# GpSimd's pattern additions of an attention kernel: int16 words with a constant instead of int32 words with a broadcast operand, and another written order

## The chip, the core and the metric

The kernel runs on one core of a Trainium2 chip. The time is the device time of one execution in microseconds, and the figure of a kernel is the median over its runs. The core has five engines that work side by side, each through its own list of instructions: TensorE (PE; its weight loads are shown apart as PEld), VectorE (DVE), ScalarE (ACT), GpSimd (POOL) and SyncE (SP), which here issues all transfers. [...]

## What is computed

The inputs are a matrix `x` of 2048 rows and 512 columns in bf16, and weights. Its normalised rows go through an attention block of 32 heads and, beside it, a gated feed-forward block; both are added to `x`:

```python
xn = _layernorm(x, axis=-1)
qkv = (xn @ wqkv).reshape(B, S, 3, H, Dh)          # H = 32, Dh = 16
p = _softmax(jnp.einsum("bhqd,bhkd->bhqk", q, k) * (Dh ** -0.5), axis=-1)
o = jnp.einsum("bhqk,bhkd->bhqd", p, v)
gate = xn @ W_gate;  gate = gate * (gate > 0)       # F = 1792
return x + o_rows @ wo + (gate * (xn @ W_up)) @ W_down
```

Most of the work is the attention: 32 heads with 2048 x 2048 scores each, whose exponentials are wanted.

## The kernel before, in words

**Tiling.** The scores are made transposed: 128 keys on the partitions and 512 queries along the free dimension, for four heads at a time. A block is 512 queries (`c4`, 4 of them) by eight heads (`gg`, 4 of them) by one half of these heads (`ee`, 2 of them), so there are 32 blocks, and each runs over 16 tiles of 128 keys (`kt`). One tile of keys in one block is four score tiles of 128 x 512 in PSUM. TensorE makes them, another engine makes exponentials of them in SBUF, and TensorE multiplies these with the values and sums over the keys (`pv_stream`, line 1255).

**Two ways to an exponential.** For a tile of keys that goes to ScalarE, two instructions of line 1376 each take two of the four score tiles (128 x 1024) through the exponential table. There are 720 of them, called units, and the program's order is told in units. The other way is `quad` (line 1323), for the tiles of keys that have a digit in `QUAD_AT` (line 67), 152 in all. There VectorE adds a bias to each score tile and rounds to int16 (line 1331, four times for one tile of keys, 608 in all); the scores have been scaled so that the bits of this integer, read as bf16, are about a power of two. That is the raw pattern, 128 x 2048 int16 words. Two more patterns are the raw one with 31 and with 81 added to each word (`SHIFTS`, line 105). All three go to TensorE as bf16, and their sum approximates the exponential.

**Who adds the shifts.** The digit in `QUAD_AT` is a mask over the two shifted patterns: a set bit gives it to GpSimd, a clear bit to VectorE. From the fourth row of the table on, rows alternate between `2...3..3..0..3..` (seven patterns for GpSimd) and `2...3..3..2..3..` (eight), until the last row (a 2 gives it one pattern, a 3 two, a 0 none). GpSimd makes 225 patterns, each in two pieces (`POOL_PIECES`, line 53), so line 1346 stands 450 times; VectorE makes the other 79 in one instruction each (line 1350). GpSimd's instruction looks at the int16 words in pairs, as int32 words, and adds a second operand, one int32 word per partition that is repeated along the row; that word holds the shift twice, as 31 x 65537 and 81 x 65537, and is made by two iotas (line 634).

```python
QUAD_AT = ("................", ".0....3.....2...", ".3...3...2...3..", "2...3..3..0..3..", "2...3..3..2..3..", ...)
SHIFTS = (0, 31, 81)
POOL_PIECES = 2
POOL_NS = 1900
```

**What else GpSimd does.** It multiplies the output of each block by the reciprocal of the softmax's sum (lines 1238 and 1243, 31 times) and does small things at the start.

**Buffers.** There are four buffers for raw patterns (`NRAW`) and five for shifted ones (`NPAT`), 16 for ScalarE's exponentials, and eight PSUM banks, of which four hold the scores of two units and four are shared by everything else.

**What sets the order.** The functions record operations in a graph (`Graph.op`, line 280) with what each reads and writes. The order on every engine is not found while the kernel is built: it is a table, packed in the text `PLAN` (line 123), which `Graph.run` (line 325) unpacks. For each of its 8245 places the table names the operation, and for operations that take a buffer, the buffer. Waits follow from reads, writes and buffers. One wait is added for the sake of SBUF: an operation marked `port` on GpSimd waits for the last VectorE operation marked `port` ahead of it in the table (line 365); VectorE's operations wait for none of GpSimd's in this way. Both line 1346 and line 1350 are marked. The durations that `Graph.op` is given (for a piece `POOL_NS / POOL_PIECES + 60`) belong to the planning of the table and decide nothing when the kernel is built.

Of the kernel before, what the change touches and what calls it, by code (L numbers as in the profile page):

```python
# [10 lines left out]
I32 = mybir.dt.int32  # L11
# [3 lines left out]
ALU = mybir.AluOpType  # L15

S = 2048
D = 512
H = 32
DH = 16  # L20
F = 1792
# [31 lines left out]
POOL_PIECES = 2  # L53
# [1375 lines left out]
```

## Time and profile before

| What | Value |
|---|---|
| median of 2 runs | 693.66 us (693.58 to 693.75) |
| the profiled execution | 690.92 us |
| its span | 689.1 us |
| TensorE's granted clock in it | 0.999 |
| busy: PE, PEld, DVE, ACT, POOL | 680.3, 355.1, 600.3, 669.8, 503.1 us |
| moved by the transfers | 35.87 MB, 52 GB/s over the span |

How to read it: the span runs from the first to the last instruction of the profiled execution, and its own time is a little longer. A busy time counts the moments in which at least one instruction of the engine was running, so two that overlap count once; the mean of one instruction in a group is its full duration, and can be longer than the time until the next one starts. In a group's row stand line, engine, operation, what it writes and reads, shape and count, then the busy time and the mean in ns, then how long the engine stood idle just before such instructions, and who ended that. The view of one line gives the shortest, the median and the longest duration, and who waited for the line. A timeline's row begins with start and length in us, and merges instructions that follow each other without a gap.

### The profile page before, as it was taken

The page shows a single profiled execution, that of the slowest core. Times are in us where ns is not written, and L with a number is a line of the kernel's source. Part 1 is how long each engine was busy: PE and PEld are TensorE (multiplying, and loading weights), DVE is VectorE, ACT ScalarE, POOL GpSimd, SP SyncE. Part 2 cuts the span into 40 slices and gives each one's busy share as a digit, 9 for nine tenths or more (in the row PEclk, how much of TensorE's full clock was granted, in tenths as well). Part 3 has the DMA queues.
Part 4 walks back from the last instruction along what each step waited for, and adds up shares of the span by engine and source line. Part 5 has one row for each costly group of instructions (what it writes and reads, how often), then busy time and mean ns, then how long its engine had stood idle before and what let it go on. Part 6 is the DMA issues. An engine that isn't in the chain of part 4 may idle for free.

```text
span 689.1 us, 45379 instructions
## 1 busy us (share of the span) xinstructions
PE 680.3 (99%) x22232; PEld 355.1 (52%) x20044; DVE 600.3 (87%) x1009; ACT 669.8 (97%) x733; POOL 503.1 (73%) x511
## 2 busy tenths in 40 slices
PE   8999999999999999999999999999999999999997
PEld 4455555554544555455544555555554455555553
DVE  9958899997999788999998787999899887988886
ACT  6999999999999999999999999999999999999994
POOL 3223669767878778968878787987878788696791
PEclk9999999999999999999999999999999999999999
DMA  7430121214111012111100104111110112131011
GB/s 215 54 74 15 51 85 31 62 44 116 35 53 45 22 53 74 40 49 46 51 25 26 29 20 118 31 43 44 44 32 22 30 58 57 61 86 31 20 30 59
DMA packets 55941, 35.87 MB, mean 52 GB/s; under 512 B 19336, under 2 KB 51784, under 8 KB 55752
## 3 DMA queue, kind: packets, MB, share of 16 engines
q1 hardware_dynamic: 55752, 32.97, 17.3%
q8 instruction: 165, 2.70, 1.6%
q14 instruction: 24, 0.20, 0.1%
HBM read 26.35 MB, written 2.35 MB: 42 GB/s over the span
## 4 chain that ended last, share of the span: by engine, by line
PE 88%; DVE 5%; ACT 4%; SPq 1%; DMA 1%; issue 0%; POOL 0%; DVEq 0%
PE ps L251 88%; ACT ring L1376 4%; DVE qd L1331 1%; DVE stats L725 1%; SPq L857 1%; DVE xn_sb L738 1%; DMA x_sb<-oT 1%; SPq L1247 0%; DMA x_sb<-in_A_x_dram 0%; DVE up_sb L1014 0%; DVE qd L1350 0%; DVE xnT L779 0%; DVE v_aug L874 0%; POOL rstd L720 0%; DVE mv L726 0%
## 5 line engine op out<-in xcount | busy, mean ns | idle before, releaser
L1376 ACT ACTIVATE ring<-ps 128x1024 bf16<-128x1024 f32 x720 | 663.5, 1100 | 3.8 <-PE ps L251 2.7
L1346 POOL TENSOR_TENSOR qd<-qd,ints 128x512 int32<-128x512 int32 x450 | 453.7, 1039 | 152.0 <-DVE qd L1350 101.8
L251 PE MATMUL ps<-qT,kT 64*32 64x512 bf16 x8192 | 451.6, 374 | 1.2 <-ACT ring L1376 0.3
L1331 DVE TENSOR_SCALAR qd<-ps 128x512 int16<-128x512 f32 x608 | 396.6, 686 | 56.9 <-PE ps L251 50.2
L251 PE MATMUL ps<-qd,v_aug 64*32 64x512 bf16 x3648 | 266.4, 375 | 0.4
L251 PE MATMUL ps<-ring,v_aug 64*32 64x512 bf16 x2880 | 241.9, 375 | 0.1
L1311 PEld LDWEIGHTS <-kT 64*32 64x32 bf16 x7732 | 158.9, 92 | 126.4 <-issue 34.2
L1283 PEld LDWEIGHTS <-v_aug 64*32 64x32 bf16 x4800 | 114.2, 91 | 79.0 <-issue 25.3
L251 PE MATMUL ps<-xnT,wgs 64*32 64x512 bf16 x1792 | 139.5, 375 | 0.1
L251 PE MATMUL ps<-xnT,wus 64*32 64x512 bf16 x1792 | 137.8, 374 | 0.0
L809 PEld LDWEIGHTS <-wus 64*32 64x32 bf16 x1792 | 43.5, 91 | 29.1 <-issue 6.7
L809 PEld LDWEIGHTS <-wgs 64*32 64x32 bf16 x1792 | 43.4, 91 | 29.1 <-issue 6.5
L251 PE MATMUL ps<-Wd,hT 64*32 64x512 bf16 x768 | 56.7, 375 | 0.5 <-DMA x_sb<-oT 0.5
L1350 DVE TENSOR_SCALAR qd<-qd 128x2048 int16<-128x2048 int16 x79 | 53.8, 693 | 2.6 <-PE ps L251 2.4
L809 PEld LDWEIGHTS <-hT 64*32 64x32 bf16 x1792 | 40.8, 92 | 26.1 <-issue 3.2
L1018 DVE SCALAR_TENSOR_TENSOR hT<-ps,up_sb 128x512 bf16<-128x512 f32 x56 | 38.4, 686 | 6.9 <-PE ps L251 6.1
L251 PE MATMUL ps<-Wk,hT 64*32 64x512 bf16 x512 | 43.9, 375 | 0.0
L251 PE MATMUL ps<-Wv,hT 64*32 64x512 bf16 x512 | 43.9, 375 | 0.0
L1014 DVE COPY up_sb<-ps 128x512 f32<-128x512 f32 x56 | 38.3, 685 | 2.2 <-PE ps L251 1.3
L251 PE MATMUL ps<-Wo_p,x_sb 64*32 64x512 bf16 x480 | 38.2, 375 | 0.0
L251 PE MATMUL ps<-xnT,Wq 64*32 64x512 bf16 x480 | 37.1, 375 | 0.0
L251 PE MATMUL ps<-xnT,Wk 64*32 64x512 bf16 x480 | 34.8, 374 | 0.2 <-DVE xnT L779 0.2
(72 smaller groups left out, 267.4 us busy)
## 6 DMA issues: line engine op xcount, KB each, us to landing
rb<-rec_scr SPq DMA_DIRECT2D x31, 256.0 KB
wus<-in_B_W_up_dram SPq DMA_DIRECT2D x38, 128.0 KB, 2.7
wgs<-in_B_W_gate_dram SPq DMA_DIRECT2D x38, 128.0 KB, 3.1
xr_sb<-in_A_x_dram SPq DMA_DIRECT2D x16, 128.0 KB, 3.1
out_dram<-xn_sb SPq DMA_DIRECT2D x16, 128.0 KB, 2.3
qT<-qf SPq DMA_DIRECT2D x120, 16.0 KB, 2.6
x_sb<-in_A_x_dram SPq DMA_DIRECT2D x8, 128.0 KB, 2.8
x_sb<-oT SPq DMA_DIRECT2D x60, 16.0 KB, 2.3
```

The lines of the kernel that those rows point to most:

```text
L251: return e.add_instruction(mybir.InstMatmult(name=e.bass.get_next_instruction_name(), engine=mybir.EngineType.PE, ins=[e.lower_ap(x), e.lo ...
L725: G.op("DVE", 580, lambda e, m=m: e.bn_stats(stats[:, m, :], xs(m)), reads=[t_xm[m]], writes=[t_st], prio=pr, order=last_xn if m == 4 else ())
L738: G.op("DVE", 320, lambda e, m=m, t=t_n: e.tensor_scalar(xn_sb[:, t.slot, :], xs(m), mv[:, m, 0:1], rstd[:, m:m + 1], op0=ALU.subtract, op ...
L809: e.ldweights(w()[rows, 32 * j:32 * j + 32], tile_position=(rows.start, 32 * j))
L1014: G.op("DVE", 603, lambda e: e.tensor_copy(up_sb[:, tup.slot, :], bank_of(tu)), reads=[tu], writes=[tup], prio=-590)
L1018: G.op("DVE", 603, lambda e: e.scalar_tensor_tensor(out=hT[:, th.slot, :], in0=bank_of(tg), scalar=0.0, in1=up_sb[:, tup.slot, :], op0=ALU ...
L1283: e.ldweights(vs(j), tile_position=(64 * half, 32 * j))
L1311: e.ldweights(ks(m), tile_position=(64 * half, 32 * m))
L1331: G.op("DVE", 601, lambda e, j=j, tx=tx: e.tensor_scalar(qd[:, tq.slot, 512 * j:512 * j + 512], ps[:, BANK[tx.slot], :], IBIAS[3], 0.0, op ...
L1346: G.op("POOL", POOL_NS / POOL_PIECES + 60, lambda e, x=x, n=n, c=slice(i * m, i * m + m): e.tensor_tensor(x().bitcast(I32)[:, c], raw().bi ...
L1350: G.op("DVE", 600, lambda e, n=n, x=x: e.tensor_scalar(x(), raw(), float(SHIFTS[n + 1]), None, op0=ALU.add), reads=[ti, tq], writes=[t], p ...
L1376: exp_ops[u] = G.op("ACT", 904, lambda e, tr=tr, k0=k0: e.activation(ring[:, tr.slot, :, :], ps[:, 4 * k0:4 * k0 + 2, :], ACTF.Exp, scale= ...
```

## The change

Two things change together. The table of order in `PLAN` is another one, with the same number of places (8245); the text of it is left out here. And the instruction of line 1346 is another: an addition of a constant that is part of the instruction, over int16 words in pieces of 1024, where it was an addition of two tensors over int32 words in pieces of 512. The number of pieces (two for a pattern, 450 in all), their bytes, their waits and `QUAD_AT` stay, as do the iotas of the shift words, which nothing reads any more.

```diff
 PLAN_OPS = 8245
 PLAN = (
...
                 if mask >> n & 1:
-                    m = 1024 // POOL_PIECES
+                    m = 2048 // POOL_PIECES
                     for i in range(POOL_PIECES):
-                        G.op("POOL", POOL_NS / POOL_PIECES + 60, lambda e, x=x, n=n, c=slice(i * m, i * m + m): e.tensor_tensor(
-                            x().bitcast(I32)[:, c], raw().bitcast(I32)[:, c], shift[:, n:n + 1].to_broadcast([128, m]), ALU.add),
+                        G.op("POOL", POOL_NS / POOL_PIECES + 60, lambda e, x=x, n=n, c=slice(i * m, i * m + m): e.tensor_scalar(
+                            x()[:, c], raw()[:, c], float(SHIFTS[n + 1]), None, op0=ALU.add),
                             reads=[ti, tq, t_shift], writes=[t] if i == 0 else [], joins=[] if i == 0 else [t], prio=u, name="p3", port=True)
```

More of the change, by code (lines that the diff above doesn't have):

```diff
@@ new lines @@
+    "@vfKu3L%hhDfg{Mig#~Y4Y?rSeLdd;Q@UKN+fR*6r8Exn(!N%#r;4wpK07GfyD>M!8C&W?f_TK~Qapsb%@ybzy79IyA8~1nys&f<Yq_3MJhwOHw!6jmT!Fc*_nskEu{~w3_qlEE3vO>L-m;&Qy4-vw"
+    "O)($QGSd!I1M!-%oo;GsD8nu5$yjdO^ahreaKj@~e|Q66`_Hl$atSTa?J!vTh~;u~A;9=Xk<Reumtv-g?H}V6Bjo0`rbUW0*AzwHx>X;~a^1Yo<qFHgy0xo(X73|x6O!Dj^n>YEa)S|eu|_xV>58Sc"
+    "VUXz*({plxP{LHisxI9sAsKzU22E2fa|~<6ZBqrq4*Mn3^F}<R)<~V~QoL_+ahO8I`|vI{LT)JJwM1IRj3N*Vjcb`ky7a$dCZ{eFQ8!{|TB&=LNvV=_4KqB)6{grFYiQts&P`zO(5B4e^&RbRit~td"
+    "iup+KVufzKYhRi15VB+%ntO<FN^3kaa!g9sJ(f0#hlxi_N-`WFuIRZ(ZY<0;-lZG#TTu*QuuS?7fO+fN2WJf*B{_5@Nz;>cr!G8Wq!bx$%h658i|x%s^(dzM<^FPS<}m{#ElASfk@;#FWjkAhST}bO"
@@ new lines @@
+    "3JXadCd-^DrgJPEErY#!c$gVDSROVi(FO>keiSbf*y%0r3dM~WFezT>BJFa6*$qNevQS2B#)VO07453J6$=V&C^GZZ!a$F)%<z`bSn4k;!SIyGFU9thnNr-`R%b@&g`_XK!-}!pHMoh$5<H|AJ)&C7"
+    "auNR|I)qoh(7(D{6CRW@MaoD?%&a`c1P;TyHrmNsmU2ceng)4{w6b%-vW8g|!K_rYCBoZhZGRd0?^Bn_4(nUp?ovkKn0PM)8vB`>dABy6>egdJ2{TPCM5PU78hWHYMxl5t!{uup1zw0Zk{i+u-UQN3"
+    "J;dd|&M!{c*+ej81Vk-*?9?^eo)0;YNuo0|fpx_!BAM}qI#vggQB^#eTNavVbB2vJ_?c}{rmSxCc*81KS!8sS&rYG4{N8pow+WAze)y1(6xY6;QnyM`YU9(0eY&KNI2m%QGuUJ;HP!RBqSW%NzM6uQ"
+    "_|&n*yzJ`t?yRRWPO1XMN+!e0T=5}$MmLs*TKk%PfO{#Ew>>I~B}VZkxLJ5!cEjyZ7=2W_(OzV=Fw2J2bW5>m2h7H2bT<=3bY1abTy~XurTK{AF!kiRkse3^Cl<9!5xrEJ@DvfyQ-<3YI{1J3t?e(9"
@@ new lines @@
+    "2^bvJFv0Y@38ZpI!$O#nd`U@)Jkou3v9<Cs-0HY?Dj7!F;NnY#y~f(xNDgPn^1#-^ZU(x^@#K1s)s4)yDDlb8XA^5|g^kjsS9HbV5eA*IH`WaVF^kmdbY`nEiL!3VFq^-jt(SJ#*6CI@(<Y8Y!V9~x"
+    "D|Uf-bZ{FnneGKJW=B~tWCJQCsCsE2H*nN!CgMsr8n}saULI;TevgQ_@ru-%+fc+U)*|J3NrZvxuzQYFhTBo#CW?9ihU>7dJ+KHRHzCmgUW-8(+nS_F_GAKmOCtB_fQsceuOZTZ+?Jwvk=ci5$u`ft"
+    "Y{tB@kVf)8len0)4fZ=s@pkEy9L}PGl6L5}gXyov&8OxhqWD&a)X&n#B-@5fHr4ThIfu_Ka%XF>um#(lP1jR&POHQF_)yLfOgDpT(GT5X{^nF<L7igF9o7t|+cT9l4O<fyxAIOg^p{FoPr0qW;YVq`"
+    "87Z-ymtoqpL{ts48iWNw+&i{dEJ06klAv2U>Anm{x7Y`_8?HUoC>CS1^H-L>ZWA!mBj!M5jHrqk2Ge{i5Zqh(K2wJUiEfe6`WL^Hvyg5#G#^m+KGA)NkZxg!Z^ulzC<QF1a_awcrsI=4|4&=D$8EE}"
@@ new lines @@
+    "8Rpm&-)P-tk1+3g=X|cDz;syUU<)vdM)x*jyWiNEENCLU=NXDGpnFM+7i2kn4wYbEnr+2<R$@5OlF7Z}gKm#4ikI8?@)(}-q{)Z5_<B|HvlLX`yba&L`MBF|0w$f&O_E}BaUCh@LrGcpsRygn&aw~6"
+    "Qsqdhb-FL{^PX|RMt-TG2_)8FC9%~)Et^NC9;(cd-D2{R=6g&;w#0CSd9{~Qf!Qa_vn+FLFa(%=$Le=JM-x8CFOTOe*tcOow@<W;Q3|@ZBK7}pRxc-jea@oWqm$x24lr;~v7TDpS+Trm%zY;COJFm`"
+    "2k-fYManz|0_$dbH(QTonOQ*I(=x9ThQYdh@}#?UXEJP@HE9C(9_X0|KGqs>k^|l5%l4q}o!=C@0~`L6JSoK-;X`@7=e()T@T6HD#uP>WZ#~&9z#NsC$2g#{4hIx7xnzmS5tr5{Yt~o=J1`deG3bZx"
+    "ZRs{Av3MTUs~tv(^md{8PD83kx4DO6yG&8Mr-cR=GfKhYrY0M+&QBHV#Dm*iR+gAsmCp4!HMI|J6}uU8<1E?k&WfEHDYF1Z6XVR*)@txx(qbp8HQ`%lnD*<67gX(1lh_2S=W}nGC@Igll+^y?-bu<N"
@@ new lines @@
+    "MO;<9hl$?9NL}H+N2C^j+f%vsu-d90n+5q|TdGDUR*FMl-#4wck?J(o2kv!m`_}(smG3ZW8>**<*Ax%`!yxsP2<~-ZN?u@}+~__>y1GyIOQnpGqEXx9hk-;$HBB4+JH>I3&*^E3zHT2!aBqQIC%q;w"
+    "^BorLp-orpGgu|nDS_o8k$J{JPO6hcb7;4Dg6_ja{&S$nZ9}>55N@?o?)_lGwo<piBGo~x57jW^<6$W$UY`S8Jq4BX`OeG3#gUWl{WQe86Sq%#{u@u8;sC);0IqWL#MVGYdGN-KGe5;R22)I4Z!}Zc"
+    "X^pX2G+cAeq#ImGG4bdglV^xA%sNPB*3he)lcRWrz|i_Y#q8l8>txpFGeF&YaBa42^C;Fhd*$ZG1_D^k@mw6*TAy#ogFK5lSficqOz4rPZ@%r?_-jxOp_b3EZ``s+T?20{4QyQ2?T%{_GTm(4im9#c"
+    "GxsU5+m&t)B{Fk;1|Z$k)@T*RhhN5rPu|G^UUc?3!A7b+V0|XWt&dwQ1m-YXzZW)rnz9WdJ~Kh8j-8s2{`d6G=MX^m0bxDm$(ip4cBT3vqBW@7vxNP=y`!$A<X`_mbDyIxZ?17&u`$Bu@HEBex?b2<"
@@ new lines @@
+    "{-0B=|D0v%DVv42w2^B3N=crP3fX)=>e0RMYMzj!0x&Ow)l)VHCFN0VilNOHQ&S+3@1SSztEX;IDYVj4=ZsItjq6NE`Rkz*&g4%}!E{yvDpys0v5cnqe^I%A5}s$#{M5V1foHkkCtlC0dHg)|$N5J="
+    "?Qe#AMd_Y{hGQ`LDqaZkyk(ggyID|kvKzQf&;LSkATL9@j|^#O8&$tn{!&G(^xSp03znvxaRn_{jkQ4j8fR*-{UnRN(r+XJb=cA>X?c7`%;@W0(G#fPz6TVTHHEtqo&x!p+ZmX68z}ZJAi?i+*0gsE"
+    "p-4i|XZ5!?ne$)y7Bl8JG<q#VlIyeIepCiBvSHOxpQh4@lhs2_58>tz;L{E?8#QYOI?`oQBK&_E6SfXp>Zyk+U+5=v;}<-d)*Bd`y(0Fdf5$Ud=QU69?|`^<9kz5>vk(~Ai@Vo`lK25=?Me!K?_~QY"
+    "jh}>Hc~ULlv@^QTvaV|u16N-MMe%R`+5zlhmpX>jn+=qhJlVbUmDY}Apu~*DJ=h~)M&A2*pXP55tcz4j-(Y`6&EaI>*XsH)U6VE*0_wMSC8>TZj{voLxTAkK47yr-gRv4x%;ESEn9UCHv%oZ$p5d8u"
@@ new lines @@
+    "1TZCeSL3X&9e#8<VQ<qccs(8{*#@rFp__lF*9!ezVSr!QaA5sS&6T7jI#&bdGh;^8^Xq`$aVqhA#A2?k2TojUNbxOw10~Vs$Ah=ooy(ycQDM}S3NL;EN_};|;GO)AtrUtXZARdybt`}$-v=cG3?WBd"
+    "!n`40%^SjdC1!YYmDEmvpUZ>e^$+9Jl<1d89&wUx&c^#`$APMjSvVOSkH>i^A<F>?^Zzb-<1kQfBUa~Jy?XpcpgnE132pLU1FGC`<#VwQH-LSJT+!7vY{9QU+2W!2l<rt9okconyW{NJD?cVZ19CK;"
+    "g$RE9K;{-Jd#*&oC&1&8b1^L0Zxs-tvbh*K7bTB>kF&!xhJ_Ie(dP<KX+=0I#g+iyR!P2Ci<3_ZT}0f1>uQNTK(jP_5&9+X1e!B97DmSS1HnJxd=&&GP)qmpJ#(QlDmlA0YORu}si84p;A<8Edq?qQ"
+    "{kFHhMNY-|$5qe&4dluF)bXbHo7md8+w2T*2ookP)$UwI24Jpx8B?8M6u*acDY6G@pX>w_ozm<bs-8m`5fA^kS$*_xnKNuRaIS~O!<!=?rOa}KFOLOl#dJsX(b^}gM+3RiB5`hM6sBA+#7<x`EztgX"
@@ new lines @@
+    "j<Hj9hDvoPyIvp{S7(iwMTwN=ZP0B$<PQXHV1MsrApv*4`bub=+3)@lrQWfgHS3eW#WVPrVEoa&#=6e!57%#qti|1T*jMg{?8zhKLC8Oa|G5K<?p24exy?i-q>sn-`mZ-n$@wHVrgvY_m3>2n@e1?X"
+    ">pV9yjoC-vJwDt$$@LtRZE=fPuZ%C*Gj!O9u8C;dyA+ah2_5gfW+lkN1Gv}=OZp<{Bk}`-*@m{8(gL@UjkTU!A}fhPt~e#p|La?|N$(<TK=^BYXRl~Vp+nLA77lQ?0rudd^Rx4L&Jdv5pbGD9IT5^@"
+    "5UMF+TfD+iSK+=FsenSZglq}L4+I7e9Y|2=-5s2}0~7@B(VO9yMzJ|xs;-v689cdE?s5eO;nXg)TivbA8X)jyvvGJhqEH;*`mIDrE41DQ)&lpDIneD2=9g$yiN6YQ^+A$2*(JH1DgX!5c%Wr|-U8T;"
+    "O`&J1uj^C=Sx?r&jw(35WgAu2NE~;Z8A!PLHXdioT#W!;V?(p;XKGL?AHlMg*j)H-a-)lfkJTLmewNf&U!m^A8WS0TZ0K0-JjZz&^j>yhHRe}1SB+I68=D@iKefD?3EhBsn_F+zx}#@Q58R3Eh}b^)"
@@ new lines @@
+    "geP0};_8yN9k7;U1gD8l>w2>|uZTe5!Vh=>;G%|%?vKb=26%o~Q!fl8aGMJ%qQMLGx<FFcTu^CI@FqJ?Y8B7#r7b&=8w;w#yCkj)UyjaimyXC+6Xe^pQF^z^e#aUzf|Z8Dzs9*`l$H$~YtL0ZTdn$("
+    "<SHlvtUg`!{7_8aMfg<<XRDn`*H;RT>girRiE6dyL{up`WFvVhuvWhn<3TWd93S6B^_x%ru6~ez@7Uk;6z~KQ_xxkgo-W@+_c-^58mn<C#e63=qxj7XY-D0KQ1TY#8aWW(($!#|=w80*O1Y4MgMm%="
+    "l}|qdy;ue}YhDeA$okwbKF#MjA*J8lZx-62uKHx}AHe=CPIqV2r1ug6+*}0(s9{dWJ?$VZsCl6_l5#WvZeB(97w7=As&_OP{~oRr4jj(XW-0i9(R%za>IwA<MzblP)wTZ@G!a;dEUuG5?`Hr*8xHu1"
+    "x<`cm_Z<4h@00&0mml32UiC8qnp50y<krZo&G*#RLn-S682C#@nOe2~q6o%jjc_FSxhdk?hll?>AAINnT5;mtt->W&6*^rbsrQmARN(u6Wwnq*AspEd2VMMoP#O1XAKM67qR5szGg;?#VKLO*!poGx"
@@ new lines @@
+    "lj8*okm|wRu;xbTKW>sj)iAJ3qqJKHW*T<mF<r45Ap?N<*IVIUrZDPNm#bW;{zV<)-k75{wvu*TfHqC=U=XET#7Vx88V6?W>sL@8hOsZ5#fqWrtE>mMw%QQWW$6d3_<C*Vrj?ZNo4MNOIY3=>{hi{Q"
+    "+HPp)SWlU84%f=zT_d1zn}AhX=cIy&ijMN@gt--Qe{4LkNEv%^4|7oM{Bf{Rxpnxe$_PD6-zAYJYTW(U@gn|si?k!%b19#HPxO0-j9WTTgD<tX|Gc4HP}EiXXkD!NaT$7VZuf>_rM8K=M|SxKC9*}h"
+    "ye<qMwtY&biVsLsCoGz(PbZUcX?~K%9RoEYIAbs}EIMk&YjP@9G$<WOkTxH=HnndVQf)qPpA`+Q^8~c$LW#Z{@#EFlcFe&qm)F-L-DoPD@L8BG>bygk-UyNGGAV#z>-J9rHe=9&s^^CMdT#w9On*O#"
+    ">arT&{0Nb=QIVQue^fm`mn}e*KTBY14lI228x`wg+?cmoWOt>UFGIrDW_ewN;OqBmAOpkO79uPx(F)ianDsR{agygJ@Z<>PZvE(VK}0*yWWTPri5?4F%kl<%BHIpJ$GBxLabze(x67BBai5C_aC*(V"
@@ new lines @@
+    "?8k?Kz@LFU^V|Tk_&K_ulGb_s56wEoV4rhGLI)E6{hmp^u9nBU?&I)k3-Ox&jhZoP)`<5M!%jU`sk~bcRIZF)2wPUp88a<U`(?le?04sVyv0or@;RtYW9;7mbeS;*UuFzllao}y>Dm`QX)AgyC=1-{"
+    "KkXzAV&4z@@K65RU)}%e_Scjq=g?$pGYWIU2=v*F-rCO~M{Ye(H+MoNY@5~k%?WhrMq6y6&CVjR)sBR;Eu92tyO2FG9vwfY`HYH7!j}wKa;z?GajGN%{WoD4Q}h5ua#n_q2?5R{jcX<)UQ#Rn@xEGl"
+    ";AgT1S@IGI&5{(rliWm}(@%=rT!vy%cBsw{WCV^b#XL57`YI4R{l^`UkZ~P`QX%|~tnNk!8xh&LhOBYr{!AxeCFjln>P`d+H=YN4#*pYW2~?GtHfF5Xsp+n@1Nx#AX?>>3RTTT{+=XOTm#E67bw`(X"
+    "+Y}np{vaA)?Yge9R4eP-&C$0G2-}akE+B@ht2OqTknpFNaJ>FyzDS;uA2PmoB|IkMmf`M{1JBSDxjN3uzX*R9)g!6+LYHUWh2}dk@J`{`k$+Y{gTRv773wmG!P{{6FW5F^Eak@M{!5b%6aIX9w<)yZ"
@@ L222 @@
+    "a;YR|fkw(3TN?dRv^WWSs)QzTt-r`DN!b{)+pPj)f1!XTJ4b-TJ0`s@yP@T3nJG+@UCb$CM&?P9AQr1KDuDEZS-i5ziz^idI{M3cRt@wv*dvT~Ec`)UrMy=p2M`gI-B2^3!;oZc%?tn)Y*YqN;s9|A"
+    "Q7q&T2(}??A;>q}4QUX?+o>9fWSXxS=qK8XpP5gTGlU7Gm%m~pmT4O)5@7UpRk9o@MY2Dcykwk|q!`>oprTROv_Liu1L91+s!FD$3Uu)k%+Da0#4llV391#@(nSwaO}?TSbWZp{Q6;V!i6JSD;t&)C"
+    "N?O4aToNEjTiQK{-bp7C-OnKEkgX2?2l|q}um")
 class Pool:
```

145 lines of the change are left out of this document (49 added, 96 removed).

## The prediction

> **What bounds the kernel now.** I read the busy shares and the costliest groups first, then ScalarE's instructions in order of time, then who waits for GpSimd, then GpSimd's own waits and runs.
>
> ```profile
> span 689.1 us, 45379 instructions
> ...
> PE 680.3 (99%) x22232; PEld 355.1 (52%) x20044; DVE 600.3 (87%) x1009; ACT 669.8 (97%) x733; POOL 503.1 (73%) x511
> ...
> L1376 ACT ACTIVATE ring<-ps 128x1024 bf16<-128x1024 f32 x720 | 663.5, 1100 | 3.8 <-PE ps L251 2.7
> L1346 POOL TENSOR_TENSOR qd<-qd,ints 128x512 int32<-128x512 int32 x450 | 453.7, 1039 | 152.0 <-DVE qd L1350 101.8
> ...
> L1331 DVE TENSOR_SCALAR qd<-ps 128x512 int16<-128x512 f32 x608 | 396.6, 686 | 56.9 <-PE ps L251 50.2
> ```
>
> PE and ACT are both nearly full, but PE's ends are modelled, so the firmer reading is ACT's: 720 exponentials with 3.8 us of idle time before them. ScalarE's timeline shows them as one chain:
>
> ```profile
> 11.18 25.27 ACT L1376 ACTIVATE ring<-ps 128x1024 bf16<-128x1024 f32 x27
> 37.22 8.36 ACT L1376 ACTIVATE ring<-ps 128x1024 bf16<-128x1024 f32 x9 [0.76 <-PE ps L251]
> 46.15 161.99 ACT L1376 ACTIVATE ring<-ps 128x1024 bf16<-128x1024 f32 x176 [0.58 <-PE ps L251]
> ...
> 473.27 205.18 ACT L1376 ACTIVATE ring<-ps 128x1024 bf16<-128x1024 f32 x222 [0.22 <-PE ps L251]
> 679.72 0.66 ACT L1149 ACTIVATE up_sb<-ps 128x256 f32<-128x256 f32 x2 [1.27 <-PE ps L251]
> ```
>
> 205.18 / 222 = 0.924 us an exponential. The first starts at 11.18, the last ends at 473.27 + 205.18 = 678.45, and 10.65 us of tail follow. The time is a start of 11 us, 720 steps of 0.924 (665.3 us), 2 us of waits and the tail. Anything else must first make this chain wait.
>
> Does anything wait for GpSimd's patterns? The view of line 1346 answers, and the view of waits says what GpSimd itself waits for:
>
> ```profile
> L1346 POOL TENSOR_TENSOR qd<-qd,ints x450: 1031/1038/1073, 34.5 to 675.7; 128x512 int32<-128x512 int32 x150
> ...
> who waited for it (us, times):
> busy tenths in 40 slices 0023659667867778868777786977768688686781
> ```
>
> ```profile
> POOL qd L1346 <- DVE qd L1350: 101.8, 48, 17.5
> POOL qd L1346 <- DVE qd L1331: 28.0, 21, 5.9
> POOL qd L1346 <- PE ps L251: 21.8, 19, 3.3
> ```
>
> The list under "who waited" is empty: no engine stood still for a piece in this execution. GpSimd itself idled 151.6 us before pieces, mostly for VectorE's adds of line 1350, which the order makes it wait for so that both don't use SBUF at once. GpSimd is cover here, not the path.
>
> **The change, part by part.** (1) Each of the 450 pieces (225 patterns of two halves) becomes an add of a constant over 1024 int16 words with one tensor operand, instead of an add over 512 int32 words with two. (2) The table of order is another. Read from the two tables: the sets of instructions are the same on every engine (PE 5566 recorded operations, ACT 732, DVE 1009, POOL 507, SP 431 transfers), the 12 filler matmuls too. ACT's order is identical; PE's first 71 operations, DVE's first 57 and last 14, and the last 4 transfers stand in the same order. The iotas of the shift constants stay, unused. Of the 431 transfers 380 stand elsewhere, by 7 places on the mean and 78 at most; I cost that at nothing, since in the waits of PE a transfer ended one wait of 0.5 us:
>
> ```profile
> PE ps L251 <- DMA x_sb<-oT: 0.5, 1, 0.5
> ```
>
> If that cover went, the price is a weight block or a packed row that comes late, some 2 us each time. Nothing is added to any queue but the new price of a piece.
>
> *Price of a piece.* What it costs in a run comes from GpSimd's timeline; the nearest rows for the new form come from its groups:
>
> ```profile
> 300.16 6.03 POOL L1346 TENSOR_TENSOR qd<-qd,ints 128x512 int32<-128x512 int32 x6 [1.91 <-DVE qd L1350]
> ...
> 319.52 7.03 POOL L1346 TENSOR_TENSOR qd<-qd,ints 128x512 int32<-128x512 int32 x7 [0.67 <-DVE qd L1331]
> 327.74 1.28 POOL L1238 TENSOR_TENSOR x_sb<-o_sb,rb 128x512 bf16<-128x512 f32 x1 [1.19 <-DVE qd L1350]
> ```
>
> ```profile
> L718 POOL TENSOR_SCALAR vare<-mv 128x4 f32<-128x4 f32 x2 | 0.5, 232 | 10.9 <-DVE mv L726 10.9
> ...
> L635 POOL CAST identf<-ident 128x128 f32<-128x128 bf16 x1 | 0.3, 337 | 0.0
> L629 POOL TENSOR_SCALAR_AFFINE_SELECT ident<-ident 128x128 bf16<-128x128 bf16 x1 | 0.3, 292 | 0.0
> L628 POOL MEMSET ident<- 128x128 bf16 x1 | 0.2, 204 | 0.0
> L636 POOL CAST selp<-ident 128x4 f32<-128x4 bf16 x1 | 0.2, 186 | 0.0
> ...
> L627 POOL MEMSET expo<- 128x4 f32 x1 | 0.1, 101 | 0.0
> ```
>
> Six old pieces take 6.03 us: (6.03 - 1.04) / 5 = 1.00 us each in a run, so a row's duration hides about 0.04 behind its neighbour. The new form's fixed part is the row of the same operation, 232 ns at 4 elements. Per element the one-operand rows give (292 - 186) / 124 = 0.855 ns (the select against the shortest copy) and (337 - 186) / 124 = 1.22 ns (the cast); the memset, which reads nothing, gives (204 - 101) / 124 = 0.83. Low end: 101 + 1020 x 0.83 = 0.95 us, 0.91 in a run. High end, at the old form's price per element, (1039 - 232) / 512 = 1.58 ns: 232 + 1020 x 1.58 = 1.84, 1.80 in a run. I take the select's slope, the one add-like row with one 16-bit operand in and out: 232 + 1020 x 0.855 = 1.10 us, 1.06 in a run. Seen the other way, an old piece reads 2 x 512 operands, a new one 1 x 1024; as many reads at about the same price.
>
> [...]
>
> *Where it lies.* In the rows of QUAD_AT from the fourth on, a block has 5 shared key tiles and 11 x 2 = 22 exponentials: 22 x 0.924 = 20.33 us. GpSimd has 14 or 16 pieces in it, by turns, and one product (1.28). At 1.06 the heavy block takes 16 x 1.06 + 1.28 = 18.2 of 20.33, so the work is still covered: 450 x 0.06 = 27 us more, out of 151.6 idle. The cover is gone where 30 c + 2 x 1.28 exceeds 40.66 over two blocks, c = 1.27; beyond that each 0.01 costs 14 pairs x 30 x 0.01 = 4.2 us.
>
> *What is late next.* A pattern ends 0.12 us later by itself, 0.4 us later at the end of a run of seven. In the new order 5 of 225 patterns have only 3 exponentials between the place of their first piece and their first reader (2 in the old), 15 have 4 or fewer (12 in the old); 3 x 0.924 = 2.77 us against 2.1 for two pieces. For these 15 I charge 0.1 us each: 1.5 us of PE, and so of ACT. The ends are -2 us (the waits that ACT has, gone) and 15 x 0.5 = 7.5.
>
> *Port.* VectorE's 79 pattern adds and GpSimd's pieces get in each other's way where they meet:
>
> ```profile
> L1350 DVE TENSOR_SCALAR qd<-qd x79: 631/684/1022, 32.8 to 677.5; 128x2048 int16<-128x2048 int16 x79
> ```
>
> ```profile
> L738 DVE TENSOR_SCALAR xn_sb<-hT,mv,rstd x8: 390/407/1225, 19.3 to 34.9; 128x512 bf16<-128x512 bf16 x8
> ```
>
> ```profile
> 34.45 1.04 POOL L1346 TENSOR_TENSOR qd<-qd,ints 128x512 int32<-128x512 int32 x1 [6.59 <-DVE qd L1350]
> ...
> 34.88 1.23 DVE L738 TENSOR_SCALAR xn_sb<-hT,mv,rstd 128x512 bf16<-128x512 bf16 x1
> ```
>
> The normalisation at 34.88 met a piece that ran from 34.45 to 35.49, and took 1.23 us against a median of 0.41. GpSimd waits for the last such add in the order, but the adds don't wait for GpSimd; where pieces grow, an add finds one still running. The longest add was 1022 - 684 = 0.34 over. At 1.06 I charge nothing: DVE idles 689 - 600 = 89 us, and 79 x 0.06 = 5 fits in it. [...]
>
> *Sum.* The profiled execution took 690.92 us (span 689.1 and 1.8 around it), 2.74 below the median of the two runs, 693.66. 690.92 + 1.5 = 692.4; at the median's level 695.2, rounded to 695.
>
> **The rivals.** *GpSimd becomes the bound (slower).* If a one-operand add runs at the cast's slope, a piece is 232 + 1020 x 1.22 = 1.48, 1.44 in a run: 420 x (1.44 - 1.27) = 71 us more, 765. At the old form's slope, 1.80: 420 x 0.53 = 223, 917. It decides from 1.27 in a run, and costs over 2% from 1.30. For it: the only long GpSimd rows here run at 1.6 ns an element and more. [...]
>
> *The adds collide (slower).* The new order's gaps fit pieces of 1.00; at 1.1 to 1.2 each of the 79 VectorE adds finds a piece running and is held as long as the worst was, 0.34: 27 us of DVE, all of it on the chain at worst: 695 + 27 = 722, likelier half, 708. Against: 89 us of DVE idle.
>
> *Pieces are shorter, or the new order better.* ACT's 2 to 3 us of waits go: 691. It can't be faster by 2% (13.9 us): 720 x 0.924 stay, and the tail's DVE order is the same.
>
> **How the numbers follow.** No change beyond 2% (piece up to 1.2 in a run): 0.65, own range 690 to 703. Pieces shorter or order better, 688 to 691: 0.06. Collisions, 703 to 722: 0.08, half of it over 2%. GpSimd the bound: 0.20, 708 up to 920. Two per cent of 693.66 is 13.9 us, about what a measurement of this kernel can tell from no change. Faster 0.01, within 0.75, slower 0.24. The range, 688 to 730, takes in the collisions and the edge of the GpSimd-bound case (0.03 of its 0.20), and leaves out 0.18.
>
> **What would show it.** Right: line 1346 at 1.0 to 1.15 us a row, POOL busy 500 to 540 us, line 1376 unchanged with under 8 us idle before it, no entry for GpSimd among those PE or DVE wait for. GpSimd bound: rows over 1.3 us, POOL over 90% busy from 60 us on, PE or PEld waiting for POOL. Collisions: line 1350's median clearly over 684 ns. Wrong in any case if ACT's exponentials change their 0.924 us step, or the start before 11.18 moves.

## The result and the profile after

The changed kernel takes 1405.41 us (two runs, 1405.24 and 1405.58) against 693.66 us: 2.0275 times as long, with a 95% interval of 2.0237 to 2.0313. The prediction was 695, its range 688 to 730. The page of the changed kernel's profile shows first where the time is:

```profile
span 1403.5 us, 45362 instructions
...
PE 873.6 (62%) x22229; PEld 413.7 (29%) x20048; DVE 627.7 (45%) x1009; ACT 704.5 (50%) x733; POOL 1306.5 (93%) x511
...
POOL 3489999999999999999999999989999999899995
PEclk9987868778687788777777878688777688788787
...
POOL 74%; PE 11%; issue 10%; DVE 4%; DVEq 0%; ACT 0%; POOLq 0%
...
L1346 POOL TENSOR_SCALAR qd<-qd 128x1024 int16<-128x1024 int16 x450 | 1255.4, 2801 | 62.9 <-DVE qd L1331 22.0
L1376 ACT ACTIVATE ring<-ps 128x1024 bf16<-128x1024 f32 x720 | 698.2, 1029 | 684.2 <-PE ps L251 681.6
L251 PE MATMUL ps<-qd,v_aug 64*32 64x512 bf16 x3648 | 357.1, 463 | 503.1 <-POOL qd L1346 502.2
```

GpSimd, which had a share of 73%, is busy for 93% of a span twice as long, and from the fourth of the 40 slices on it is nearly full. A piece takes 2801 ns on the mean, not 1039. The matmuls that read the patterns now stand idle for 503 us before they start, nearly all of it for GpSimd, and the exponentials, which stood idle for 3.8 us, do so for 684. The chain that ended last is GpSimd's. In the view of line 1346 the list of those who wait, empty before, is filled:

```profile
L1346 POOL TENSOR_SCALAR qd<-qd x450: 2761/2768/3413, 34.5 to 1384.4; 128x1024 int16<-128x1024 int16 x150
...
who waited for it (us, times):
  PE ps L251: 502.2, 152
  DVE qd L1331: 43.3, 8
```

The busy time of the pieces grew by 1255.4 - 453.7 = 802 us, and the span by 714: the difference came out of the idle time that GpSimd had before its pieces, 152 us then and 63 now.

### The profile page after: what moved, and what is told of

Its sections match the earlier page's. It is cut to its first block, busy times and chain, and to the rows that moved or that the text cites. A ratio compares the mean times of both kernels' runs of the same rounds, so it can differ in the third digit from the quotient of the medians.

```text
span 1403.5 us, 45362 instructions
## 1 busy us (share of the span) xinstructions
PE 873.6 (62%) x22229; PEld 413.7 (29%) x20048; DVE 627.7 (45%) x1009; ACT 704.5 (50%) x733; POOL 1306.5 (93%) x511
## 4 chain that ended last, share of the span: by engine, by line
POOL 74%; PE 11%; issue 10%; DVE 4%; DVEq 0%; ACT 0%; POOLq 0%
POOL qd L1346 72%; PE ps L251 11%; DVE qd L1331 2%; POOL x_sb L1238 1%; DVE qd L1350 1%; POOL oT L1243 1%; DVE stats L725 1%; PE ps L906 0%; DVE xn_sb L738 0%; DVE up_sb L1014 0%; DVE v_aug L874 0%; DVE hT L1018 0%; DVE qT L950 0%; DVE xnT L779 0%; DVE o_sb L1209 0%
## 5 line engine op out<-in xcount | busy, mean ns | idle before, releaser
L1346 POOL TENSOR_SCALAR qd<-qd 128x1024 int16<-128x1024 int16 x450 | 1255.4, 2801 | 62.9 <-DVE qd L1331 22.0
L1376 ACT ACTIVATE ring<-ps 128x1024 bf16<-128x1024 f32 x720 | 698.2, 1029 | 684.2 <-PE ps L251 681.6
L251 PE MATMUL ps<-qd,v_aug 64*32 64x512 bf16 x3648 | 357.1, 463 | 503.1 <-POOL qd L1346 502.2
L251 PE MATMUL ps<-qT,kT 64*32 64x512 bf16 x8192 | 591.0, 449 | 15.5 <-DVE qd L1331 8.3
L1311 PEld LDWEIGHTS <-kT 64*32 64x32 bf16 x7720 | 184.7, 106 | 524.2 <-issue 452.9
L251 PE MATMUL ps<-ring,v_aug 64*32 64x512 bf16 x2880 | 286.7, 445 | 0.6 <-issue 0.4
L1283 PEld LDWEIGHTS <-v_aug 64*32 64x32 bf16 x4816 | 133.3, 107 | 147.1 <-issue 101.9
L251 PE MATMUL ps<-xnT,wgs 64*32 64x512 bf16 x1792 | 173.1, 446 | 2.3 <-DVE qd L1331 2.3
L251 PE MATMUL ps<-xnT,wus 64*32 64x512 bf16 x1792 | 172.4, 444 | 1.4 <-DVE qd L1331 1.3
L1350 DVE TENSOR_SCALAR qd<-qd 128x2048 int16<-128x2048 int16 x79 | 71.1, 910 | 11.0 <-PE ps L251 10.9
```

The source lines that it names most:

```text
L251: return e.add_instruction(mybir.InstMatmult(name=e.bass.get_next_instruction_name(), engine=mybir.EngineType.PE, ins=[e.lower_ap(x), e.lo ...
L1283: e.ldweights(vs(j), tile_position=(64 * half, 32 * j))
L1311: e.ldweights(ks(m), tile_position=(64 * half, 32 * m))
L1346: G.op("POOL", POOL_NS / POOL_PIECES + 60, lambda e, x=x, n=n, c=slice(i * m, i * m + m): e.tensor_scalar(x()[:, c], raw()[:, c], float(SH ...
L1350: G.op("DVE", 600, lambda e, n=n, x=x: e.tensor_scalar(x(), raw(), float(SHIFTS[n + 1]), None, op0=ALU.add), reads=[ti, tq], writes=[t], p ...
L1376: exp_ops[u] = G.op("ACT", 904, lambda e, tr=tr, k0=k0: e.activation(ring[:, tr.slot, :, :], ps[:, 4 * k0:4 * k0 + 2, :], ACTF.Exp, scale= ...
```

## The experiments

Two questions were open. Is it the price of a piece alone, or also the new order? And what makes the price? A third came from the prediction itself: had the price been the 1.06 us in a run that it reckoned, would the rest of its sum have held? The price of a piece is what GpSimd spends on one of the 450; where it is given as busy time, it is the busy time of the rows of the pieces over 450, which for the old piece is 453.7 / 450 = 1.01 us, close to the 1.00 in a run. The knee is the price up to which dearer pieces cost no time.

**The old order with the new addition.** The text of `PLAN` is that of the kernel before; line 1346 is the changed one.

```diff
-(PLAN of the changed kernel)
+(PLAN of the kernel before)
```

> The old table of order with the new additions over 1024 int16 words. Price theory (the doubling is the price of the 450 additions, 2.77 us a row, and the order does nothing): 1390 to 1420 us, rows of line 1346 at 2.77 us again, GpSimd over 90% busy. Order theory (the new order itself costs more than 2% because it puts patterns and readers badly): clearly less, below 1375 us, with GpSimd waiting more than the 63 us that it idles before pieces now.

Measured: 1421.36 us, 2.0472 times the kernel before (2.0425 to 2.0519).

```profile
L1346 POOL TENSOR_SCALAR qd<-qd 128x1024 int16<-128x1024 int16 x450 | 1252.3, 2793 | 84.9 <-DVE qd L1350 37.8
```

The old order doubles the time as well, so the new order isn't the cause. The time lies 1.4 us above the span that the price theory gave. It is 16 us slower than with the new order, the two intervals don't meet, and GpSimd's idle time before pieces is 22 us longer: once GpSimd is the bound, the new order keeps it a little busier.

**The new order with the old addition.**

```diff
-                    m = 2048 // POOL_PIECES
+                    m = 1024 // POOL_PIECES
...
-e.tensor_scalar(x()[:, c], raw()[:, c], float(SHIFTS[n + 1]), None, op0=ALU.add)
+e.tensor_tensor(x().bitcast(I32)[:, c], raw().bitcast(I32)[:, c], shift[:, n:n + 1].to_broadcast([128, m]), ALU.add)
```

> The new table of order with the old additions over 512 int32 words. Price theory: 690 to 697 us, within 0.5% of the kernel before, rows of line 1346 at 1.04 us, under 8 us of idle time before ScalarE's exponentials. Order theory: over 707 us.

Measured: 692.36 us, 0.9975 times the kernel before (0.996 to 0.999).

```profile
L1376 ACT ACTIVATE ring<-ps 128x1024 bf16<-128x1024 f32 x720 | 664.5, 1121 | 5.1 <-PE ps L251 4.2
L1346 POOL TENSOR_TENSOR qd<-qd,ints 128x512 int32<-128x512 int32 x450 | 453.5, 1039 | 149.6 <-DVE qd L1350 60.6
```

The price theory holds. The order by itself is worth a quarter of a per cent, on the good side. That is little: over the three series of runs here the kernel before has medians from 692.35 to 694.02 us, which lie as far apart.

**Two lengths of the new addition.** The pieces of a pattern are 512 and 1536 words.

```diff
-c=slice(i * m, i * m + m)
+c=slice(512 * i, 512 + 1536 * i)
```

> The changed kernel with the two pieces of each pattern cut unevenly, 512 and 1536 int16 words, so that two lengths give the fixed part and the price per word of the same instruction. Per-word theory (232 ns fixed, as in the row of four elements, and 2.48 ns a word): rows of 1.50 and 4.04 us, time 1395 to 1430. Fixed-part theory (0.855 ns a word as I predicted, and 1.9 us of start-up in every instruction): rows of 2.33 and 3.20 us, time 1395 to 1430 as well. The rows decide, not the time.

Measured: 1429.93 us (one run). GpSimd's groups by shape, with the mean in ns behind the busy time:

```profile
L1346 POOL TENSOR_SCALAR qd<-qd 128x1536 int16<-128x1536 int16 x225 | 922.7, 4103 | 36.9 <-DVE qd L1350 14.7 <-PE ps L251 11.4 <-DVE qd L1331 1.3
L1346 POOL TENSOR_SCALAR qd<-qd 128x512 int16<-128x512 int16 x225 | 344.2, 1533 | 43.0 <-DVE qd L1331 22.3 <-DVE qd L1350 6.0 <-PE ps L251 5.1
```

(4103 - 1533) / 1024 = 2.51 ns a word, and 1533 - 512 x 2.51 = 248 ns fixed. Both rows are near those of the per-word theory. The fixed part is as predicted (232); the price per word is three times the 0.855 that I took.

**Four forms side by side.** In the changed kernel, by pattern `n` and piece `i`; shortened, with `o` for the shifted pattern, `r` for the raw one and `c` for the 1024 words of the piece:

```diff
+if (n, i) == (0, 0): e.tensor_scalar(o[:, c], r[:, c], float(SHIFTS[n + 1]), None, op0=ALU.add)
+if (n, i) == (0, 1): e.tensor_copy(o[:, c], r[:, c])
+if (n, i) == (1, 0): e.tensor_scalar(o.bitcast(BF16)[:, c], r.bitcast(BF16)[:, c], 1.5, None, op0=ALU.mult)
+if (n, i) == (1, 1): e.tensor_tensor(o.bitcast(BF16)[:, c], r.bitcast(BF16)[:, c], r.bitcast(BF16)[:, c], ALU.add)
```

> The changed kernel with four forms over 1024 16-bit words side by side, 112 or 113 of each: the addition of a constant over int16 as it is, a plain copy of int16, a multiplication of bf16 by a constant, and an addition of two bf16 tensors. The copied quarter leaves the addition out, and the two bf16 forms compute something else; only the prices count. Loop theory (the constant form has a slow loop on GpSimd whatever the type): int16 constant 2.77, bf16 constant 2.77, copy 1.0 to 1.4, two bf16 tensors 2.3 to 2.6 us. Type theory (16-bit integers have to be converted to float and back, and that is slow): int16 constant 2.77 and copy 2.0 or more, bf16 constant 1.0 to 1.4 us. The time should follow GpSimd's sum: 1403 less 112 us for each microsecond that a form is shorter than 2.77, so 1150 to 1300.

Measured: 1129.64 us (one run). GpSimd makes the first pattern of a tile of keys less often than the second, so there are 90 of each of the first two forms and 135 of the others, not 112 or 113. The views of the four lines give the shortest, the median and the longest in ns:

```profile
L1347 POOL TENSOR_SCALAR qd<-qd x90: 2768/2775/3216, 40.9 to 1107.3; 128x1024 int16<-128x1024 int16 x90
```

```profile
L1349 POOL COPY qd<-qd x90: 1027/1037/1492, 36.4 to 1103.5; 128x1024 int16<-128x1024 int16 x90
```

```profile
L1351 POOL TENSOR_SCALAR qd<-qd x135: 2761/2774/3242, 38.0 to 1104.5; 128x1024 bf16<-128x1024 bf16 x135
```

```profile
L1352 POOL TENSOR_TENSOR qd<-qd x135: 1886/1893/2435, 34.6 to 1110.1; 128x1024 bf16<-128x1024 bf16 x135
```

The type theory falls: int16 and bf16 cost the same with a constant, and the int16 copy is short. The copy reads and writes the same 1024 words in 1.04 us, as long as an old piece, so moving the words need not cost 2.77. And two tensor operands (here the same raw pattern twice) added in 1.89 us are cheaper than one tensor and a constant, which no theory had so low (2.3 at least). The time is below the 1150 to 1300 that were expected, and the rows account for it: 90 x (2.775 - 1.037) + 135 x (2.774 - 1.893) = 275 us less than the changed kernel's span of 1403.5 gives 1128, and the span is 1127.9.

**Four more one-operand forms.** Shortened as above; `d` is the piece's 512 words of four bytes, `s` the shift.

```diff
+if (n, i) == (0, 0): e.tensor_scalar(o.bitcast(FP32)[:, d], r.bitcast(FP32)[:, d], 1.0, None, op0=ALU.mult)   # 512 words
+if (n, i) == (0, 1): e.tensor_scalar(o[:, c], r[:, c], expo[:, 0:1], None, op0=ALU.add)
+if (n, i) == (1, 0): e.tensor_scalar(o[:, c], r[:, c], s, 0.0, op0=ALU.add, op1=ALU.max)
+if (n, i) == (1, 1): e.tensor_scalar(o.bitcast(I32)[:, d], r.bitcast(I32)[:, d], 1.0, None, op0=ALU.mult)    # 512 words
```

> The changed kernel with four other one-operand forms: 512 float words times 1.0, 1024 int16 words plus a value read from a column per partition, 1024 int16 words with two steps (add the shift, then the larger of that and zero), and 512 int32 words times 1.0. The two forms that multiply by 1.0 and the column form leave the right shift out; only the prices count. Per-word theory (the loop costs 2.5 ns a word whatever the width and whatever the constant's source, and always walks both steps): 1.50, 2.77, 2.77 and 1.50 us. Step theory (each arithmetic step is paid for): the two-step form at 3.5 us or more. Per-byte theory: 2.77 us for the 512-word forms as well. Time with the per-word theory near 1130 us, GpSimd's busy time plus about 100.

Measured: 1239.16 us (one run), in the same order of forms:

```profile
L1347 POOL TENSOR_SCALAR qd<-qd x90: 1482/1496/2332, 43.1 to 1220.1; 128x512 f32<-128x512 f32 x90
```

```profile
L1349 POOL TENSOR_SCALAR qd<-qd,expo x90: 2839/2847/3788, 36.0 to 1213.6; 128x1024 int16<-128x1024 int16 x90
```

```profile
L1351 POOL TENSOR_SCALAR qd<-qd x135: 3619/3634/4161, 39.4 to 1216.4; 128x1024 int16<-128x1024 int16 x135
```

```profile
L1352 POOL TENSOR_SCALAR qd<-qd x135: 1480/1493/1922, 34.5 to 1221.9; 128x512 int32<-128x512 int32 x135
```

The price goes by words, not by bytes: 512 words of four bytes take 1.49 us, 1024 words of two 2.77, and with 248 ns fixed that is 2.4 to 2.5 ns a word for both. Where the constant comes from matters little (2847 ns from a column, 2768 from the instruction). A second step costs (3634 - 2768) / 1024 = 0.85 ns a word more, so the step theory is right on that point, and the per-word theory's "always walks both steps" is wrong; that is also why the time lies 109 us over what was expected (135 two-step pieces x 0.87 us = 117).

**A little of the new form.** Each piece is an int32 addition of 504 words and a constant addition of the last 16 int16 words.

```diff
+e.tensor_tensor(o.bitcast(I32)[:, c], r.bitcast(I32)[:, c], shift[:, n:n + 1].to_broadcast([128, 512 - k]), ALU.add)
+e.tensor_scalar(o[:, d], r[:, d], float(SHIFTS[n + 1]), None, op0=ALU.add)     # the last 2 k words; k = 8
```

> New order; each piece as an int32 addition of 504 words and, behind it, a constant addition of the last 16 int16 words, so that GpSimd's price of a piece is raised by a known small amount with the sums unchanged: about 0.99 + 0.23 = 1.21 to 1.22 us in a run. Knee theory (the prediction's: hidden until 1.27): 690 to 697 us. Sum theory (the time is GpSimd's busy time plus about 100 us once that passes 690, as in the runs with the slow form): 450 x 1.215 + 50 + 100 = 697 us and more, with PE waiting for GpSimd in many places.

Measured: 755.55 us, 1.0904 times the kernel before (1.0868 to 1.0941): over both theories. In this kernel's GpSimd groups the short instruction's mean is 295 ns, though its median is 252 and its longest 1266:

```profile
L1346 POOL TENSOR_TENSOR qd<-qd,ints 128x504 int32<-128x504 int32 x450 | 463.1, 1029 | 81.0 <-DVE qd L1331 29.8 <-DVE qd L1352 21.4 <-PE ps L251 18.7
L1347 POOL TENSOR_SCALAR qd<-qd 128x16 int16<-128x16 int16 x450 | 132.9, 295 | 12.2
```

A piece costs (463.1 + 132.9) / 450 = 1.32 us of busy time, not 1.22, and GpSimd still idles 93 us before pieces, while the view of waits has PE waiting for it 58 times, 44.1 us in total:

```profile
PE ps L251 <- POOL qd L1347: 44.1, 58, 2.0
```

At 1.32 the prediction's own price beyond the knee, 4.2 us for each 0.01 over 1.27, gives 21 us more, some 713. The measured time is 42 us over that. So either the knee comes earlier than 1.27 or the time rises faster behind it; this run alone doesn't say which.

**Some more of it.** The same with k = 64, which is 448 int32 words and 128 int16 words.

> The same with 448 int32 words and 128 int16 words a piece: about 0.89 + 0.51 = 1.40 us in a run, beyond the knee. Knee theory with 4.2 us for each 0.01 us over 1.27: 691 + 55 = 746 us. Sum theory: 450 x 1.40 + 50 + 100 = 780 us.

Measured: 833.24 us, 1.2032 times the kernel before (1.1965 to 1.2099), again over both theories. GpSimd is busy for 713.8 us here against 627.9 in the run above: 86 us more work, 78 us more time.

**The predicted price, without the new form.** New order and old addition, with instructions cut in two to add one fixed part each: first one piece of each pattern, then both, then both in four. (`parts` is the number of instructions for piece `i`.)

```diff
+m = 512 // parts                          # parts = (2, 1)[i], then 2, then 4
+for q in range(parts):
+    c = slice(512 * i + m * q, 512 * i + m * q + m)
+    ins = e.tensor_tensor(o.bitcast(I32)[:, c], r.bitcast(I32)[:, c], shift[:, n:n + 1].to_broadcast([128, m]), ALU.add)
```

> New order, old addition; the first piece of each pattern is cut into two instructions of 256 int32 words, so that the same sums cost one more fixed part: on the average of both pieces about 1.00 + 0.135 / 2 = 1.07 us in a run, the price that the prediction had put on the new form. Cover theory (the prediction's: what is under 1.2 us lies in GpSimd's idle time): 690 to 695 us, within 0.3% of the new order with whole pieces (692.4). Early-knee theory (the line through the runs at 1.22 and 1.40 us, extended, meets the flat part near 1.14 us, and lateness shows before that): 694 to 705 us.

Measured: 695.93 us, 1.0042 times the kernel before (1.0023 to 1.0062).

```profile
PE 682.0 (98%) x22229; PEld 355.6 (51%) x20048; DVE 605.0 (87%) x1009; ACT 673.3 (97%) x733; POOL 535.7 (77%) x736
...
L1380 ACT ACTIVATE ring<-ps 128x1024 bf16<-128x1024 f32 x720 | 667.0, 1092 | 8.1 <-PE ps L251 6.3
```

The price is (264.0 + 231.4) / 450 = 1.10 us of busy time (its groups of 256 and 512 words), a little over the 1.06 in a run that was predicted, and the time is near the predicted 695. But the cover theory's 690 to 695 is missed by 0.9 us, and its 0.3% as well: against the kernel before, 1.0042 here and 0.9975 with whole pieces make 0.67%, or 4.6 us. The early-knee theory's 694 to 705 holds. ACT's idle time before exponentials is 8.1 us, 3 more than with whole pieces. PE waits for GpSimd only twice, 0.5 us in total. What did grow is VectorE's pattern adds, by 59.6 - 54.8 = 4.8 us; first the row with whole pieces, then the row of this run:

```profile
L1350 DVE TENSOR_SCALAR qd<-qd 128x2048 int16<-128x2048 int16 x79 | 54.8, 706 | 0.7 <-PE ps L251 0.7
```

```profile
L1354 DVE TENSOR_SCALAR qd<-qd 128x2048 int16<-128x2048 int16 x79 | 59.6, 766 | 1.0 <-PE ps L251 1.0
```

> The same with both pieces cut in two: about 1.13 to 1.14 us in a run. Cover theory: 690 to 697 us. Early-knee theory: 695 to 720 us, with PE waiting for GpSimd in tens of places.

Measured: 708.57 us, 1.0229 times the kernel before (1.0205 to 1.0253).

```profile
PE 684.4 (97%) x22229; PEld 358.2 (51%) x20048; DVE 613.7 (87%) x1009; ACT 676.6 (96%) x733; POOL 569.8 (81%) x961
...
PE 55%; POOL 22%; DVE 14%; ACT 6%; issue 2%; DMA 0%; DVEq 0%; POOLq 0%
...
L1348 POOL TENSOR_TENSOR qd<-qd,ints 128x256 int32<-128x256 int32 x900 | 520.4, 617 | 101.0 <-DVE qd L1354 44.4
...
L1354 DVE TENSOR_SCALAR qd<-qd 128x2048 int16<-128x2048 int16 x79 | 70.1, 898 | 0.4 <-PE ps L251 0.3
```

```profile
PE ps L251 <- POOL qd L1348: 5.7, 16, 0.7
```

520.4 / 450 = 1.16 us a piece, and already 2.3% slower, with 101 us of GpSimd's idle time unused and GpSimd on 22% of the chain. The early-knee theory has the time right and the waits only in part: PE waits for GpSimd 16 times, 5.7 us in total, not in tens of places. The span is 705.7 us, 15.0 more than with whole pieces (690.7), and VectorE's pattern adds take 70.1 - 54.8 = 15.3 us more. So two readings fit the first rise of the time: patterns that come late, and adds that take longer beside GpSimd's work. The trace has places of the second kind. Here an add takes 2.50 us beside GpSimd, TensorE then waits 0.46 us for it, and ScalarE soon after 0.39 us for TensorE:

```profile
539.06 1.28 POOL L1238 TENSOR_TENSOR x_sb<-o_sb,rb 128x512 bf16<-128x512 f32 x1
...
539.53 2.50 DVE L1354 TENSOR_SCALAR qd<-qd 128x2048 int16<-128x2048 int16 x1
...
540.30 1.17 POOL L1348 TENSOR_TENSOR qd<-qd,ints 128x256 int32<-128x256 int32 x2
...
542.08 0.38 PE L251 MATMUL ps<-qd,v_aug 64*32 64x512 bf16 x4 [0.46 <-DVE qd L1354]
...
543.20 2.01 ACT L1380 ACTIVATE ring<-ps 128x1024 bf16<-128x1024 f32 x2 [0.39 <-PE ps L251]
```

On the chain that ended last, GpSimd has 22% here and VectorE 14%, against 0 and 5% with whole pieces. Cutting an instruction in two brings more of both, and no run here keeps them apart.

Both pieces cut in four, 128 int32 words an instruction:

> [...] If the price alone decides: 810 to 850 us. If the constant form has another effect beside its price: below 800 us.

Measured: 817.20 us, 1.1794 times the kernel before (1.1747 to 1.1842), in the expected span of "the price alone decides". GpSimd's busy time is 708.9 us, close to the 713.8 of the run with k = 64 (833 us), though no constant form is in it; what is left between the two times is 16 us. At this price (659.7 / 450 = 1.47 us of busy time a piece) it is mostly the patterns that come late: PE waits for GpSimd 83 times, 80.2 us in total. VectorE's pattern adds take longer still, with a median of 883 ns against 684:

```profile
L1354 DVE TENSOR_SCALAR qd<-qd x79: 676/883/3357, 33.3 to 804.5; 128x2048 int16<-128x2048 int16 x79
```

Put in order of GpSimd's busy time, all ten and the changed kernel lie near one curve:

| Kernel | GpSimd busy, us | Time, us |
|---|---|---|
| new order, old addition | 503.0 | 692.4 |
| one piece cut in two | 535.7 | 695.9 |
| both cut in two | 569.8 | 708.6 |
| 504 + 16 words | 627.9 | 755.6 |
| both cut in four | 708.9 | 817.2 |
| 448 + 128 words | 713.8 | 833.2 |
| four forms | 1028.1 | 1129.6 |
| four more forms | 1141.1 | 1239.2 |
| old order, new addition | 1303.5 | 1421.4 |
| changed kernel | 1306.5 | 1405.4 |
| uneven pieces | 1314.4 | 1429.9 |

It is nearly flat up to some 540 us (33 us of work for 3.5 of time), bends, and from about 630 on nearly every microsecond of work is one of time: 1405.4 - 755.6 = 650 us of time for 1306.5 - 627.9 = 679 of work. Some kernels lie off this by up to 20 us, as the one with uneven pieces does.

## Why the prediction was wrong

**The price of a piece: the step that failed.** The prediction took "the select's slope" and came to 1.10 us, with 1.84 as the high end. It measured 2.77, beyond the high end. The fixed part was right (248 ns against 232 taken). Wrong was the reasoning "as many reads at about the same price". Moving the words does cost what I took: the copy reads and writes 1024 words in 1.04 us, (1037 - 186) / 1020 = 0.83 ns a word. But the constant form costs 2.5 ns a word for any type and width tried (int16, bf16, int32, fp32; 512 to 1536 words), so 1.7 ns a word are beyond what a copy of the words costs. What GpSimd does in them, no run shows. Nor did the old form's price per word bound it from above: one operand and a constant is dearer than two operands (2.77 against 1.89 us at 1024 words). The row of the very operation, 232 ns at four elements, holds 10 ns of that price and could not show it; and an instruction that only shared the word "one operand" stood in for it.

**The rival that came true.** "GpSimd becomes the bound" had a chance of 0.20, and its signs were the right ones: rows over 1.3 us, GpSimd over 90% busy, PE waiting for it. Its size wasn't: its dearest case was 917, since the cast's 1.22 ns a word and the old form's 1.58 are both well under 2.51. Its formula at the measured 1255.4 / 450 = 2.79 us gives 693.66 + 420 x 1.52 = 1332, 73 short of 1405.41. The 30 pieces of the first and last blocks, left out of it, are also slowed (30 x 1.5 = 45 us); for the other 28 us no run gives a reason.

**The cover: nearly right at the predicted price, wrong about where it ends.** With a price of about that size the kernel takes 695.9 us, inside the prediction's own range of 690 to 703. That it lies so near 695 is in part luck: the sum had 1.5 us for late patterns and nothing for the order, and the runs show 4.6 us for the dearer pieces and 1.7 us gained by the order. The end of the cover did not hold: the prediction put it at 1.27 us, from the work of two blocks against their exponentials, and at 1.16 the time is already up by 2.3%. The step that failed is that GpSimd's idle time counted as room anywhere. In that run 101 us of it stay unused, 79 of them (44.4 and 34.5) while GpSimd waits for VectorE's adds and evictions. Whether the time rises there because patterns come late or because VectorE's adds take longer stays open, as said above. That the few pattern buffers keep GpSimd from working ahead wasn't tried; the waits that PE ends, as those for a buffer still being read would be, are the smallest part, the other 21.9 us.

**The order.** Costed at nothing, and worth 0.25% with the old price, little more than nothing. With the new price it is worth 16 us, 1.1%.

**The collisions.** Real, but not the cause of the doubling: the changed kernel's adds of line 1350 have a median of 694 ns against 684. Their mean is 910, so 79 x 0.22 = 17 us more of VectorE, which is 45% busy there. At the predicted price the prediction charged them nothing, since VectorE's idle time would take them in; the run at 1.10 us has 4.8 us more of them and 4.6 us more time. Its likelier figure for this rival, 708, is what the kernel with both pieces cut takes, which doesn't show that the adds are the cause there.

## What to carry to other kernels

Price an operation on GpSimd by a long row of the same operation. A row of four elements, 232 ns here, showed little but the fixed part (248 ns by the two lengths), and the count of operands didn't rank the forms: a copy took 1.04 us for 1024 words, two tensors 1.89, a tensor and a constant 2.77. Idle time of an engine isn't all cover: of 150 us here some 30 were nearly free. GpSimd's busy share said little of how near the knee was (73% before, 77% with 0.4% more time, 81% with 2.3%), so where a price is uncertain, a cheap way to find the knee is to cut its instructions in two and see whether the time moves.

## What the runs showed of the hardware

GpSimd's constant form costs 2.5 ns a word for one step (4103 ns for 1536 words, 1533 for 512) and 0.85 ns more for a second one, by words and not by bytes (1493 ns for 512 int32 words). Two tensor operands cost less, 1893 ns for 1024 words against 2774, and a copy 1037.

VectorE's add over 2048 int16 words, 684 ns on the median before, can take longer beside GpSimd's work. In the traces of the kernel before and of the changed kernel, 70 and 7 of the 79 adds ran beside no GpSimd instruction, and none of these took over 696 ns. Of the others 4 and 37 took over 700, up to 1022 and 1566, while 5 and 35 took no more than that. The changed kernel's pieces, 2768 ns on the median, took up to 3413, and each one over 2830 ran beside such an add. In the run with both pieces cut in four the longest add took 3357 ns, as long as eight of GpSimd's instructions there (401 ns on the median).

TensorE's granted clock fell with its share of busy time, though the set of its instructions stayed the same: 1.00 at 92 to 99% busy, 0.99 at 87%, 0.97 at 86%, 0.87 at 72%, 0.83 at 67% and 0.79 at 62% in the changed kernel, whose matmuls on the patterns have a mean of 463 ns (in the result above) against 375 before:

```profile
L251 PE MATMUL ps<-qd,v_aug 64*32 64x512 bf16 x3648 | 266.4, 375 | 0.4
```

The lower clock doesn't seem to add to the time where GpSimd is the bound: span less GpSimd's busy time is 99.8, 96.2 and 97.0 us at clocks of 0.87, 0.83 and 0.79. That was not tried by itself.
